# A saturating add in place of add and row ReLU in the inner feed-forward product, with every engine's queue put in a new order

## The chip, the cores and the metric

The kernel runs on one core of one Trainium2 chip. The metric is the device time of one execution in microseconds (us), the median of several runs. A core has TensorE (PE, matrix products into the PSUM banks; its weight loads are shown as PEld), VectorE (DVE), ScalarE (ACT), GpSimd (POOL) and SyncE (SP, which here only issues transfers).

## The reference

Two linear-attention blocks and two feed-forward blocks follow one another on x of 2048 rows by 512 columns; all tensors are bf16.

```python
def _A_ref(x, wqkv, wo):                      # 32 heads of 16
    qkv = (x @ wqkv) ...
    phi = lambda t: jnp.where(t > 0, t + 1, jnp.exp(t)) + 1e-6
    pq, pk = phi(q), phi(k)
    kv = jnp.einsum("bhsd,bhse->bhde", pk, v)
    z = jnp.einsum("bhsd->bhd", pk)
    num = jnp.einsum("bhqd,bhde->bhqe", pq, kv)
    den = jnp.einsum("bhqd,bhd->bhq", pq, z)[..., None] + 1e-6
    return (num / den) ... @ wo
def _B_ref(x, w1, w2):                        # w1 512x1376, w2 1376x512
    h = jnp.maximum(jnp.einsum("bsd,df->bsf", x, w1), 0)
    return jnp.einsum("bsf,fd->bsd", h, w2)
x = x + _A_ref(_layernorm(x), A_wqkv, A_wo)
x = x + _B_ref(_layernorm(x), B_w1, B_w2)     # then both once more
```

## The kernel before

The rows are 16 tiles of 128, taken in four chunks `t` of four tiles. Layers 0 and 2 are attention, layers 1 and 3 feed-forward. Everything stays in SBUF between layers.

**The queues.** The kernel is a list of about 1,640 small steps (`_Graph.add`), each with a name such as `pqs3_0`, its layer in front (`2.pqs3_0`), an engine, and the keys it reads and writes. A planner (`_list_schedule`) gives each engine its list. With `WINDOW` 1 on every engine, and the engine of each movable step fixed by an entry of `HINTS` whose name ends in `!`, an engine's list is simply its steps sorted by the index at which they were made plus their entry in `HINTS`. A queue is worked strictly in that order: a step that waits holds all behind it. Waits are on semaphores: a step waits for the steps that wrote what it reads or that read what it overwrites.

**Attention.** LayerNorm (`ln_stats`, `ln_norm`) gives `xn`; `tr…` are transposing transfers issued by SP into `Tb`, and for the first six tiles `trp…`/`trev…` transpose on PE and copy out. `kproj`, `qproj`, `qh` and, for many chunks, the Strassen form `k7`/`q7` (seven products for eight) make k and q; `_lin`, `_exp`, `_em`, `_phi` make phi of them; `g…`, `kv…`, `kvmask`, `m…` make the per-head matrix `Mf`, copied out by `gev…` and `mev…`. `wvless0` to `wvless3` subtract from the value weights their last row, which the load `ld_wvl` broadcast to all partitions. The denominator of chunk t is `den t` on PE, then `lnd t` (logarithm, L1222) and `rdc t` (exponential, L1224) on ACT, then four SP transfers `spread t_0..3` (L1234) that copy the reciprocals over the partitions, then two DVE products `pqs t_0`, `pqs t_2` (L1242) that scale q. `fin` (output product, 512 columns wide) of the chunk's four tiles waits for both; `resid` on DVE adds x.

**Feed-forward.** `b_h7` makes h of a chunk by a Strassen-Winograd form: products `h1` to `h7` for 2 or 1 pairs of column blocks at once (three groups `cs` per chunk: two wide, 512 columns of a PSUM bank, and one narrow, 256), results saved by ACT (`hv…`) or seeded into a second bank (L702). Two quarters of h are a bank's content clipped (`hc11`, `hc21`, ACT L1431 or DVE L1432); the other two, `hc12` and `hc22`, are a bank plus a saved product. The function `add` puts these two into the left and right half of one row of `big` (L1443, DVE) and, behind the second, clips the whole row in place: `hc22r` (ACT L1452 or DVE L1453). The last 96 columns are `hr`, clipped by `hrrelu` into a buffer that `ms_hr` set to zero on POOL, and transposed by `trh`. `b_out_sums` and `b_out` form the second product the same way; `p…` are its products.

Of the kernel before, what the change touches and what calls it, by code (L numbers as in the profile page):

```python
# [6 lines left out]

# [55 lines left out]
HINTS = {"0.aqsum1": -44, "0.aqsum1!": 0, "0.aqsum2": -5, "0.aqsum2!": 0, "0.aqsum3": -114, "0.aqsum3!": 0, "0.aqsum4": 0,  # L63
         "0.aqsum4!": 0, "0.as1": -12, "0.as1_2": -16, "0.as1_2!": 0, "0.as1_3": -37, "0.as1_3!": 0, "0.as2_2": 4,
         "0.as2_2!": 0, "0.as2_3": -26, "0.as2_3!": 0, "0.as3": -8, "0.as3_2": 30, "0.as3_2!": 0, "0.as3_3": 3,
         "0.as3_3!": 0, "0.as4_2": 17, "0.as4_2!": 0, "0.as4_3": -22, "0.as4_3!": 0, "0.as_h1": -11, "0.as_h2": -8,
         "0.as_id": 2, "0.bnag0": -4, "0.bnag1": -8, "0.bnag10": 37, "0.bnag11": 34, "0.bnag12": 8, "0.bnag13": 8,
         "0.bnag14": 7, "0.bnag15": -18, "0.bnag2": 1, "0.bnag3": 1, "0.bnag4": 5, "0.bnag5": 25, "0.bnag6": 6,
         "0.bnag7": 3, "0.bnag8": 36, "0.bnag9": 27, "0.bnst0": -6, "0.bnst1": -10, "0.bnst10": 27, "0.bnst11": 29,
         "0.bnst12": 2, "0.bnst13": -2, "0.bnst14": 2, "0.bnst15": -26, "0.bnst2": -3, "0.bnst3": -3, "0.bnst4": -2,  # L70
         "0.bnst5": 16, "0.bnst6": 2, "0.bnst7": -4, "0.bnst8": 23, "0.bnst9": 16, "0.den0": 11, "0.den1": 26,
         "0.den2": 17, "0.den3": -32, "0.fill0": 3, "0.fin0_0": -3, "0.fin0_2": 10, "0.fin10_0": -88, "0.fin11_0":
         -97, "0.fin12_0": -138, "0.fin13_0": -147, "0.fin14_0": -170, "0.fin15_0": -166, "0.fin1_0": -8, "0.fin1_2":
         4, "0.fin2_0": 4, "0.fin2_2": 0, "0.fin3_0": 6, "0.fin3_2": -6, "0.fin4_0": -8, "0.fin5_0": -28, "0.fin6_0":
         -12, "0.fin7_0": -36, "0.fin8_0": -95, "0.fin9_0": -87, "0.fnorm0": 1, "0.fnorm0!": 0, "0.fnorm1": -3,
         "0.fnorm1!": 0, "0.fnorm10": 43, "0.fnorm10!": 0, "0.fnorm11": 39, "0.fnorm11!": 0, "0.fnorm12": 17,
         "0.fnorm12!": 0, "0.fnorm13": 20, "0.fnorm13!": 0, "0.fnorm14": 10, "0.fnorm14!": 0, "0.fnorm15": 11,
         "0.fnorm15!": 0, "0.fnorm2": 6, "0.fnorm2!": 0, "0.fnorm3": 7, "0.fnorm3!": 0, "0.fnorm4": 35, "0.fnorm4!":
         0, "0.fnorm5": 54, "0.fnorm5!": 0, "0.fnorm6": 10, "0.fnorm6!": 0, "0.fnorm7": 6, "0.fnorm7!": 0, "0.fnorm8":
         47, "0.fnorm8!": 0, "0.fnorm9": 49, "0.fnorm9!": 0, "0.g0_0_0": 40, "0.g0_0_1": 8, "0.g0_0_2": -3,  # L80
         "0.g0_0_3": -31, "0.g0_1_0": 43, "0.g0_1_1": 14, "0.g0_1_2": 6, "0.g0_1_3": -28, "0.g0_2_0": 101, "0.g0_2_1":
         64, "0.g0_2_2": 23, "0.g0_2_3": -24, "0.g0_3_0": 12, "0.g0_3_1": 4, "0.g0_3_2": -20, "0.g0_3_3": -20,
         "0.g1_0_0": -11, "0.g1_0_1": -9, "0.g1_0_2": -9, "0.g1_0_3": -7, "0.g1_1_0": -9, "0.g1_1_1": -4, "0.g1_1_2":
         -3, "0.g1_1_3": 0, "0.g1_2_0": -71, "0.g1_2_1": -3, "0.g1_2_2": -1, "0.g1_2_3": -1, "0.gev0_0": -26,
         "0.gev0_0!": 0, "0.gev0_2": -22, "0.gev0_2!": 0, "0.gev1_0": -2, "0.gev1_0!": 0, "0.gev1_2": 2, "0.gev1_2!":
         0, "0.gevz": -12, "0.gevz!": 0, "0.k0_exp": -53, "0.k0_lin": -44, "0.k10_exp": -12, "0.k10_lin": -15,
         "0.k11_em": 10, "0.k11_exp": -22, "0.k11_lin": -38, "0.k11_phi": 21, "0.k12_em": -31, "0.k12_exp": -37,
         "0.k12_lin": -21, "0.k12_phi": -11, "0.k13_em": -44, "0.k13_exp": -47, "0.k13_lin": -37, "0.k13_phi": -28,
         "0.k14_em": -45, "0.k14_exp": -50, "0.k14_lin": -55, "0.k14_phi": -16, "0.k15_em": -63, "0.k15_exp": -67,
         "0.k15_lin": -62, "0.k15_phi": -24, "0.k1_em": 53, "0.k1_exp": -39, "0.k1_lin": -32, "0.k1_phi": 78,  # L90
         "0.k2_exp": -34, "0.k2_lin": -36, "0.k3_em": 55, "0.k3_exp": -29, "0.k3_lin": 6, "0.k3_phi": 58, "0.k4_exp":
         -46, "0.k4_lin": -15, "0.k5_em": 20, "0.k5_exp": 9, "0.k5_lin": 7, "0.k5_phi": 36, "0.k6_exp": -43,
         "0.k6_lin": -35, "0.k7_em": 1, "0.k7_exp": -17, "0.k7_lin": -32, "0.k7_phi": 40, "0.k8_exp": 24, "0.k8_lin":
         32, "0.k9_em": 28, "0.k9_exp": -18, "0.k9_lin": -21, "0.k9_phi": 33, "0.kproj0_0": -58, "0.kproj0_1": -56,
         "0.kproj10": -51, "0.kproj11": -47, "0.kproj12": -42, "0.kproj13": -53, "0.kproj14": -63, "0.kproj15": -73,
         "0.kproj1_0": -56, "0.kproj1_1": -52, "0.kproj2": -48, "0.kproj3": -42, "0.kproj4": -51, "0.kproj5": -16,
         "0.kproj6": -54, "0.kproj7": -48, "0.kproj8": -22, "0.kproj9": -30, "0.kv0_0": -25, "0.kv0_1": -24,
         "0.kv0_2": -24, "0.kv0_3": -20, "0.kv1_0": 1, "0.kv1_1": 1, "0.kv1_2": 4, "0.kv1_3": 4, "0.kvmask0": -22,
# [24 lines left out]
         "0.qc7_2_12_add": 22, "0.qc7_2_12_em": 30, "0.qc7_2_12_exp": 26, "0.qc7_2_12_phi": 33, "0.qc7_2_21_em": 51,
# [1858 lines left out]
```

## Time and profile before

| | |
|---|---|
| time, median of 3 runs (range) | 261.85 us (261.5 to 262.0) |
| span of the profiled execution, first to last instruction | 260.5 us |
| what the median has beside that span | 1.3 us |
| DVE busy | 230.8 us, 89% of the span, 572 instructions |
| ACT busy | 206.3 us, 79%, 446 instructions |
| POOL busy | 60.0 us, 23%, 163 instructions |
| transfers | 22.46 MB, mean 86 GB/s |

The profile is one execution. Times in its views are us from the start of the span; "mean" is ns of one instruction. [...]

### The profile page before, as it was taken

The numbers are of one execution on the slowest core, as the hardware profiler recorded it, in microseconds if no ns is written. First come the engines' busy times: TensorE is split into PE (matmuls) and PEld (weight loads), VectorE is DVE, ScalarE is ACT, GpSimd is POOL, SyncE is SP. The second block draws the span as 40 slices with busy tenths as digits, with TensorE's granted clock in tenths as the row PEclk, the third lists the DMA queues.
The fourth block names the chain that finished last, engine by engine and source line by source line (L and its number), as shares of the span: only waits on it lengthen the run. The fifth ranks groups of instructions, "written<-read, shape, count | busy, mean of one in ns | idle before, by whom it ended". The sixth has DMA issues, their size and how long they took to land.

```text
span 260.5 us, 5876 instructions
## 1 busy us (share of the span) xinstructions
PE 255.2 (98%) x2165; PEld 198.3 (76%) x2176; DVE 230.8 (89%) x572; ACT 206.3 (79%) x446; POOL 60.0 (23%) x163
## 2 busy tenths in 40 slices
PE   7999999999999999999999999999999999999995
PEld 3554577744788988889888878674388989888884
DVE  5999997799999999999989999858999998876684
ACT  4999999689999969999998899766899928853100
POOL 4100000037844015341420430003777000000000
PEclk9999999999999999999999999999999999999999
DMA  6767950754343062222130040057251414300104
GB/s 195 288 161 140 324 183 18 178 122 94 65 89 64 17 86 44 40 42 43 31 72 0 4 81 1 3 136 174 59 102 38 83 23 126 58 20 3 81 3 161
DMA packets 46268, 22.46 MB, mean 86 GB/s; under 512 B 35904, under 2 KB 44704, under 8 KB 46240
## 3 DMA queue, kind: packets, MB, share of 16 engines
q1 hardware_dynamic: 45968, 21.83, 34.8%
q10 hardware_dynamic: 272, 0.26, 0.4%
q8 instruction: 17, 0.28, 0.4%
q14 instruction: 11, 0.09, 0.1%
HBM read 7.14 MB, written 2.10 MB: 35 GB/s over the span
## 4 chain that ended last, share of the span: by engine, by line
PE 82%; DVE 5%; DMA 4%; SPq 4%; ACT 3%; issue 1%; DVEq 0%
PE ps L960 81%; SPq L1234 4%; DMA big<-rdc 3%; DVE xres L967 3%; DVE big L1242 1%; ACT lnd L1222 1%; DMA xin<-in_A_x_dram 1%; PE ps L919 1%; ACT rdc L1224 1%; DVE bst L851 0%; ACT big L1073 0%; DVE xin L1391 0%; PE ps L846 0%; ACT escr L1090 0%; ACT GT L1144 0%
## 5 line engine op out<-in xcount | busy, mean ns | idle before, releaser
L975 ACT ACTIVATE sqscr<-xres 128x512 bf16<-128x512 f32 x48 | 29.7, 621 | 4.4 <-DVE xres L967 3.0
L960 PE MATMUL ps<-w,big 128*128 128x256 bf16 (+1 forms) x256 | 32.6, 272 | 0.0
L960 PE MATMUL ps<-big,xn 128*128 128x256 bf16 (+1 forms) x221 | 31.6, 287 | 0.3
L702 ACT ACTIVATE ps<-ps 128x512 f32<-128x512 f32 (+1 forms) x41 | 22.7, 563 | 11.1 <-PE ps L960 11.1
L960 PE MATMUL ps<-Mf,big 128*128 128x512 bf16 x125 | 28.8, 379 | 0.7 <-DVE big L1242 0.5
L960 PEld LDWEIGHTS ps<-w,big 128*128 128x128 bf16 (+1 forms) x256 | 24.9, 98 | 3.1
L960 PEld LDWEIGHTS ps<-big,xn 128*128 128x128 f16 x224 | 21.5, 98 | 6.1 <-issue 0.7
L1443 DVE TENSOR_TENSOR big<-ps,escr 128x512 bf16<-128x512 f32 (+1 forms) x38 | 22.7, 600 | 3.6 <-PE ps L960 2.3
L960 PEld LDWEIGHTS ps<-Mf,big 128*128 128x128 bf16 x128 | 12.0, 98 | 15.8 <-DVE big L1242 2.0
L960 PE MATMUL ps<-Tb,w 128*128 128x256 f16 x160 | 23.7, 273 | 0.0
L960 PE MATMUL ps<-xn,xin 128*128 128x256 f16 x160 | 23.2, 273 | 0.0
L960 PE MATMUL ps<-xn,w 128*128 128x256 f16 x160 | 22.4, 273 | 0.0
L873 POOL TENSOR_SCALAR mean<-s 128x2 f32<-128x2 f32 x24 | 8.4, 350 | 56.0 <-DVE xres L967 53.5
L899 ACT ACTIVATE xn<-xres,nbias,rstd 128x512 f16<-128x512 f32 x26 | 20.7, 816 | 0.7 <-POOL nbias L883 0.6
L1462 ACT ACTIVATE escr<-ps 128x512 f32<-128x512 f32 (+1 forms) x38 | 19.2, 536 | 2.4 <-PE ps L960 2.3
L1431 ACT ACTIVATE big<-ps 128x512 bf16<-128x512 f32 (+1 forms) x38 | 19.0, 533 | 1.9 <-PE ps L960 1.8
L960 PE MATMUL ps<-wqkv,Tb 128*128 128x512 bf16 (+1 forms) x93 | 19.7, 342 | 0.1
L881 POOL TENSOR_TENSOR rstd<-veps,nhalf 128x2 f32<-128x2 f32 x24 | 18.4, 768 | 5.1 <-DVE veps L879 4.5
L960 PEld LDWEIGHTS ps<-Tb,w 128*128 128x128 bf16 x160 | 15.5, 98 | 2.5 <-DVE w L1391 0.4
L960 PE MATMUL ps<-w,Tb 128*128 128x96 bf16 (+2 forms) x176 | 17.3, 224 | 0.0
L960 PEld LDWEIGHTS ps<-xn,w 128*128 128x128 bf16 x160 | 15.4, 98 | 2.0
L960 PEld LDWEIGHTS ps<-xn,xin 128*128 128x128 bf16 x160 | 15.2, 98 | 2.0 <-DVE xres L967 0.2
(146 smaller groups left out, 626.1 us busy)
## 6 DMA issues: line engine op xcount, KB each, us to landing
big<-rdc SPq DMA_DIRECT2D x32, 128.0 KB, 2.7
w<-in_B_w_dram SPq DMA_DIRECT2D x1, 1376.0 KB, 7.2
w<-in_B_w_dram SPq DMA_DIRECT2D x1, 1280.0 KB, 10.4
xin<-in_A_x_dram SPq DMA_DIRECT2D x2, 512.0 KB, 6.5
wqkv<-in_A_wqkv_dram SPq DMA_DIRECT2D x3, 256.0 KB, 4.9
xin<-in_A_x_dram SPq DMA_DIRECT2D x4, 128.0 KB, 3.1
xin<-in_A_x_dram SPq DMA_DIRECT2D x2, 256.0 KB, 4.9
wqkv<-in_A_wqkv_dram SPq DMA_DIRECT2D x1, 512.0 KB, 4.1
```

Source lines behind the costliest of these rows:

```text
L702: g.add(ACT, lambda e: e.activation(psv[:, b, 0:w], psv[:, src, 0:w], ACTF.Identity), [("ps", src)], [("ps", b)], C_ACT_PSUM if w == 512 e ...
L873: g.add(POOL, lambda e: e.tensor_scalar(mean[:, sl], s1[:, sl], -INV_D, None, ALU.mult), [("s1", i) for i in tl], [("mean", i) for i in tl ...
L881: g.add(POOL, lambda e: e.tensor_tensor(rstd[:, sl], veps[:, sl], nhalf[:, 0:n], ALU.pow), [("veps", lo), ("nhalf",)], [("rstd", i) for i ...
L899: (ACT, lambda e: e.activation(xn[:, i, :], src, ACTF.Identity, scale=rstd[:, i:i + 1], bias=nbias[:, i:i + 1]), C_ACT_SB_AP)],
L919: last = e.transpose(psb()[:, 128 * q:128 * q + 128], xn[:, i, 128 * c:128 * c + 128], ident[:])
L960: last = e.matmul(o, l, r, start=st, stop=sp, skip_group_check=skip)
L967: g.add(DVE, lambda e: e.scalar_tensor_tensor(xres[:, i, :], psv[:, b, :], 0.0, src, ALU.add, ALU.add, accum_out=s1[:, i:i + 1]), [("ps", ...
L975: g.add(ACT, lambda e: e.activation(sqscr[:, q, :], xres[:, i, :], ACTF.Square, scale=math.sqrt(INV_D), accum_out=s2[:, i:i + 1]), xr(i), ...
L1234: dma(lambda e, j=j, u=u: e.dma_start(unit_ap(u), rdc[32 * j:32 * j + 32, t, :].unsqueeze(1).broadcast_to([32, 4, 512])), [("rdc", t)], [( ...
L1431: g.add_flex([(ACT, lambda e: e.activation(ap, src(), ACTF.Relu), C_ACT_PSUM if w == 512 else 270.0), (DVE, lambda e: e.tensor_scalar(ap, ...
L1443: g.add(DVE, lambda e: e.tensor_tensor(ap, sh(psv[:, bank, 0:w]), sh(other()), ALU.add), [("ps", bank)] + okeys + ([] if first else bk), q ...
L1462: g.add(ACT, lambda e, w=w: e.activation(q[:, 0:w], psv[:, bank, 0:w], ACTF.Identity), [("ps", bank)], key, C_ACT_PSUM if len(cs) == 2 els ...
```

## The change

In `add`, the DVE addition becomes one instruction `TENSOR_ADD_SAT`, which gives max(min(a + b, s0), s1); with s0 the largest f32 and s1 zero it is the sum, clipped. There is then no `hc22r`.

```diff
+from concourse import dve_ops
...
+        SPREADS = ((0,), (1,), (2,))
+        H_SAT = True
+        FMAX = 3.4028234663852886e38
...
-        FIRST_ACT_TILES = 4
+        RSTD_ACT = (0, 1, 2, 3, 6, 8, 12)
+        PE_TILES = 6
...
-                g.add_flex([(DVE, f, C_DVE_NORM_BF)],
+                g.add_flex([(DVE, f, C_DVE_NORM_BF)] + ([(POOL, f, C_POOL_NORM)] if i >= PE_TILES else []),
...
+                if H_SAT:
+                    g.add(DVE, lambda e: e._custom_dve(dve_ops.TENSOR_ADD_SAT, out=ap, in0=sh(psv[:, bank, 0:w]), in1=sh(other()), s0=FMAX, s1=0.0),
+                          [("ps", bank)] + okeys + ([] if first else bk), qk + (bk if first else []),
+                          C_DVE_PSUM if len(cs) == 2 else 335.0, name="%s_%d_%d" % (name, t, cs[0]))
+                    return
                 g.add(DVE, lambda e: e.tensor_tensor(ap, sh(psv[:, bank, 0:w]), sh(other()), ALU.add),
```

`RSTD_ACT`, `PE_TILES` and `SPREADS` have values that give the same steps as before; the merged form of the spreads that `a_spread` now allows is not used. `fnorm` of a later tile may go to POOL, and `fnorm9` does. `wvless` may go to POOL, but all four stay on DVE.

The rest of the diff replaces the whole table `HINTS` (1,907 entries become 1,796), and with it all five queues. 66 movable steps change engine. Among them, in layer 0: `trev2` and `gev0_0` from ACT to DVE, `mev0` from ACT to DVE and `mev1` back, `fnorm9` from DVE to POOL; in layer 2 `var4` and `veps4` from DVE to POOL; of the clips `hc11` and `hc21`, twelve wide and one narrow go from ACT to DVE and six wide and one narrow the other way. Stretches of the queues that differ (index plus hint, sorted):

| queue | before | after |
|---|---|---|
| PE, layer 0 | den0, g0_0_3, g0_1_3, g0_2_2, g0_2_3, q7_3_4, kv0_0, kv0_1, kv0_2, den2, den1 | den0, g0_0_3, g1_2_0, g0_2_3, g0_1_3, q7_3_4, den2, den1, g1_2_1, kv0_0, kv0_1, kv0_2 |
| ACT, layer 0 | lnd0, rdc0, gev0_0, gev0_2, qc7_3_22_exp, lnd2, rdc2, qc7_3_21_lin, lnd1, qc7_3_21_exp, rdc1 | lnd0, rdc0, gev0_2, lnd2, rdc2, qc7_3_22_exp, lnd1, rdc1 |
| DVE, layer 0 | pqs0_0, mev1, pqs2_2, aksum1, kvmask1, aksum2, aksum3, pqs2_0, pqs1_0, pqs1_2, resid1 | mev0, qc7_3_21_em, pqs2_2, qc7_3_21_phi, aksum1, kvmask1, aksum2, pqs2_0, aksum3, pqs1_0, pqs1_2, resid1 |
| DVE, layer 2 | pqs2_0, resid4, resid5, nbias0, resid7, resid6, var4, pqs3_0, veps4, nbias2, pqs3_2 | pqs2_0, resid4, resid5, nbias0, resid6, resid7, pqs3_0, pqs3_2, nbias2 |
| ACT, layer 2 | gevz, …, lnd0, rdc0, lnd1, rdc1, lnd2, rdc2 | the same |
| SP, layer 0 | ld_wv0, ld_wvl, tr2_1, tr2_0, tr3_1, tr3_0, ld_wo | ld_wv0, tr2_1, tr2_0, tr3_1, tr3_0, ld_wvl, ld_wo |
| DVE, layer 0 | the first step that reads ld_wvl is at place 51 (wvless3) | at place 73 (wvless2) |
| POOL, layer 0 | ms_hr among the first nine steps | ms_hr between nbias2 and norm3 |

Up to `wvless2` the DVE's new list holds, against the old list up to `as1_2`: in addition trev2, aqsum2, four sums (as1_2, as2_2, as1_3, as4_2), four wide `_em` (k5, k11, q1_1, q0_3), one single `_em` (k14) and four wide `_phi` (k5, k7, q0_1, k11); and not any more fnorm9, aqsum3 and wvless3.

More of the change, by code (lines that the diff above doesn't have):

```diff
@@ L60 @@
 WINDOW = {PE: 1, ACT: 1, DVE: 1, POOL: 1, SP: 1}
-HINTS = {"0.aqsum1": -44, "0.aqsum1!": 0, "0.aqsum2": -5, "0.aqsum2!": 0, "0.aqsum3": -114, "0.aqsum3!": 0, "0.aqsum4": 0,
[302 rows of a table removed]
+HINTS = {"0.aqsum1": -54, "0.aqsum2": -52, "0.aqsum3": 52, "0.aqsum4": 70, "0.as1": 46, "0.as1_2": -23, "0.as1_3": -51, "0.as2_2": -17, "0.as2_3": -7,
[219 rows of a table added]
 class _Op:
@@ L1116, in wv_less_last @@
             for m in range(4):
-                g.add(DVE, lambda e, m=m: e.tensor_tensor(wqkv[:, m, 2 * D:3 * D], wqkv[:, m, 2 * D:3 * D], wvl[:], ALU.subtract),
-                      [("wv0",), ("wvl",)], [("wv", m)], 335.0, name="wvless%d" % m)
+                f = (lambda e, m=m: e.tensor_tensor(wqkv[:, m, 2 * D:3 * D], wqkv[:, m, 2 * D:3 * D], wvl[:], ALU.subtract))
+                g.add_flex([(DVE, f, 335.0), (POOL, f, C_POOL_ADD)], [("wv0",), ("wvl",)], [("wv", m)], name="wvless%d" % m)
         def ones_col(lo, n):
@@ L1228, in rb_unit, with a_spread @@
             return 32 + 4 * j + t
-        def a_spread(t, first_layer):
-            late = 500.0 if first_layer and t == 0 else 0.0
+        def a_spread(t, n=1):
             for j in range(4):
                 u = rb_unit(t, j)
-                dma(lambda e, j=j, u=u: e.dma_start(unit_ap(u), rdc[32 * j:32 * j + 32, t, :].unsqueeze(1).broadcast_to([32, 4, 512])),
-                    [("rdc", t)], [("big", u)], 650.0, "spread%d_%d" % (t, j), issue=620.0, late=late)
+                dma(lambda e, j=j, u=u: e.dma_start(big[:, u * 512:(u + n) * 512],
+                                                    rdc[32 * j:32 * j + 32, t:t + n, :].rearrange("p n k -> p (n k)").unsqueeze(1)
+                                                    .broadcast_to([32, 4, 512 * n])),
+                    [("rdc", t + k) for k in range(n)], [("big", u + k) for k in range(n)], 650.0 * n, "spread%d_%d" % (t, j), issue=620.0)
         def a_pqs(t):
@@ L1676, in ln_first @@
             for i in range(4 * t, 4 * t + 4):
-                if t < FIRST_PE_CHUNKS and i < 6:
+                if i < PE_TILES:
                     ln_stats_first(i, [("xn", i - 2)] if 2 <= i < 4 else [])
@@ L1684, in ln_first @@
             if t == 1:
-                ln_part_first(6, 8)
-                ln_norm(6, True)
-                ln_norm(7, True)
-                tr_dma(1, 1)
+                for i in range(PE_TILES, 8, 2):
+                    ln_part_first(i, i + 2)
+                    ln_norm(i, True)
+                    ln_norm(i + 1, True)
+                    tr_dma(1, i // 2 - 2)
             if t >= FIRST_PE_CHUNKS:
@@ L1762, in pq @@
                         a_zc()
-                        for u in range(NCH - 1):
-                            a_den(u)
-                            a_spread(u, first_layer)
+                        for grp in SPREADS:
+                            for u in grp:
+                                a_den(u)
+                            a_spread(grp[0], len(grp))
                         if ("q", t) in A7[layer]:
@@ L1815, in p2 @@
                         a_den(NCH - 1)
-                        a_spread(NCH - 1, first_layer)
+                        a_spread(NCH - 1)
                         a_pqs(2)
```

2 lines of the change are left out of this document (1 added, 1 removed), and 521 rows, old and new, of the table HINTS.

## The prediction

> **What bounds the kernel now.** I read the page's busy lines and chain first, then the stages table over the two long feed-forward stretches, then PE's timeline.
>
> ```profile
> PE 255.2 (98%) x2165; PEld 198.3 (76%) x2176; DVE 230.8 (89%) x572; ACT 206.3 (79%) x446; POOL 60.0 (23%) x163
> ...
> PE 82%; DVE 5%; DMA 4%; SPq 4%; ACT 3%; issue 1%; DVEq 0%
> ```
>
> ```profile
> 70.00:150.00 80.00, 80.00 (x762) 71.14 (x760) 76.89 (x210) 72.79 (x155) 25.00 (x66) 1.00 0.24 45
> 190.00:250.00 60.00, 60.00 (x588) 53.62 (x587) 51.32 (x109) 38.37 (x82) 8.50 (x21) 1.00 0.24 54
> ```
>
> ```profile
> 19.89 1.03 PE L960 MATMUL ps<-wqkv,Tb 128*128 128x512 bf16 x4
> 167.28 1.03 PE L960 MATMUL ps<-big,xn 128*128 128x256 bf16 x8
> 61.70 2.15 PE L960 MATMUL ps<-Mf,big 128*128 128x512 bf16 x8
> 182.83 3.63 PE L960 MATMUL ps<-Mf,big 128*128 128x512 bf16 x16 [0.18 <-DVE big L1242]
> 186.76 3.41 PE L960 MATMUL ps<-Mf,big 128*128 128x512 bf16 x15 [0.30 <-DVE big L1242]
> ```
>
> ```profile
> L960 PE MATMUL ps<-Mf,big 128*128 128x512 bf16 x125 | 28.8, 379 | 0.7 <-DVE big L1242 0.5
> ```
>
> PE busy is the first column pair, the granted clock stands third from the end (1.00). In both stretches, where all the saturating adds lie, PE is busy throughout: 140 of 140 us. To see whether "busy" is real work I take start-to-start distances. Four 512-column products last 1.03 us and one is counted 0.379, so the distance is (1.03 - 0.379)/3 = 0.217 us; eight 256-column products give, with 0.27 for one, (1.03 - 0.27)/7 = 0.109. 588 products in 60 us are 0.102 on average, with the narrow ones among them. So PE streams there, and nothing is waited for.
>
> Where does PE wait? At 182.83 it is idle 0.18 us, at 186.76 0.30. As a product is counted 0.379 - 0.216 = 0.16 beyond its pace, PE really loses 0.34 and 0.46. At 61.70 eight products should last 7 x 0.217 + 0.379 = 1.90; they last 2.15, so 0.25 is lost too. These three, 1.05 us in all, are what a new order can win here. All three are behind `pqs`, DVE L1242.
>
> **The adds and the clips.**
>
> ```profile
> L1443 DVE TENSOR_TENSOR big<-ps,escr 128x512 bf16<-128x512 f32 x26 | 17.7, 684 | 1.9 <-PE ps L960 1.6
> L967 DVE SCALAR_TENSOR_TENSOR xres<-ps,xres 128x512 f32<-128x512 f32 x16 | 10.3, 686 | 0.1
> L1452 ACT ACTIVATE big<-big 128x1024 bf16<-128x1024 bf16 x7 | 7.4, 1059 | 0.9 <-DVE big L1443 0.9
> L1453 DVE TENSOR_SCALAR big<-big 128x1024 bf16<-128x1024 bf16 x9 | 3.8, 417 | 0.0
> L1452 ACT ACTIVATE big<-big 128x512 bf16<-128x512 bf16 x3 | 1.9, 640 | 2.3 <-DVE big L1443 2.3
> L1453 DVE TENSOR_SCALAR big<-big 128x512 bf16<-128x512 bf16 x5 | 1.4, 285 | 0.0
> L1432 DVE TENSOR_SCALAR big<-ps 128x512 bf16<-128x512 f32 x7 | 4.8, 682 | 0.0
> ```
>
> Removed are 24 row clips: ACT 7.4 + 1.9 = 9.3 us, DVE 3.8 + 1.4 = 5.2 us. The queues give part of it back: a net six wide bank clips go to DVE, 6 x 0.68 = 4.1 us by the L1432 row, and leave ACT. So ACT loses its 9.3 us and six clips more, and DVE about 1 us. On the time this is worth nothing by itself: PE, 140 of 140 us busy, does as many products as before. What the clips cost was hidden behind PE, and so is what replaces them. The sums `ssum` of `b_out_sums`, which read the finished rows, can start a clip earlier; they feed `p…` products, for which PE did not wait in either stretch, so that too is worth nothing there.
>
> The saturating add has no row. From below: an add that costs less than the plain one is excluded as far as rows go, since plain and two-operation instructions of this shape from PSUM have one price, 684 and 686 ns. From above: add and clip one behind the other, 684 + 682 = 1.37 us, 0.68 more. I take 0.68 us, no extra, because the nearest row is that of two operations in one pass. The point from which it decides: in 70 to 150 DVE has 80 - 76.9 = 3.1 us free; of the 5.2 us freed some 2.2 lie there (of layer 1's clips four wide and two narrow were DVE's), and of the bank clips that change engine a net two wide come and one narrow goes, some 1.0 more to do. That leaves 4.3 us for 16 wide and 8 narrow adds, about 20 wide ones: 0.2 us each. Above 0.9 us per wide add DVE becomes the bound.
>
> **The new order in layer 0.** The chain in order of time (start, us, what):
>
> ```profile
> 45.18 0.61 ACT lnd L1222
> ...
> 51.53 2.60 DMA big<-rdc
> ...
> 54.15 0.69 DVE big L1242
> ...
> 61.11 1.66 DVE big L1242 x2
> ...
> 62.81 2.76 PE ps L960 x12
> ```
>
> ```profile
> 44.30 0.50 PE L960 MATMUL ps<-GT,wqkv 128*128 128x128 bf16 x6
> 44.73 0.61 PE L960 MATMUL ps<-big,Zc 128*32 128x512 bf16 x8
> 43.39 1.05 ACT L1154 ACTIVATE GT<-ps 128x512 bf16<-128x512 f32 x2
> 44.34 0.71 ACT L1090 ACTIVATE escr<-big,nbexp 128x512 bf16<-128x512 bf16 x1
> 52.72 2.12 DVE L1242 TENSOR_TENSOR big<-big 128x1024 bf16<-128x1024 bf16 x3
> ```
>
> `den2` moves ahead of `kv0_0` to `kv0_2`, six products, so it starts at 44.30, not 44.73. `lnd2` moves ahead of `gev0_0` (now on DVE) and of `qc7_3_22_exp`, the steps at 43.39 and 44.34, so ACT is free for it. `rdc2` and the eight SP issues behind it come 0.43 earlier, and so do the last landing (54.13) and `pqs1_2`. But DVE, in order, gains only what it waits: three `pqs` at a pace of 0.61 would end after 2 x 0.61 + 0.69 = 1.91 and take 2.12, so 0.21. From there `resid` and `pqs3` run without a hole to 62.77, and PE's 0.25 falls to 0.04. Gain 0.21, bounds 0 (another step is late) and 0.25. What DVE takes on there, `gev0_0`, costs up to 0.68 (as the L1432 row, a read of a full bank); it lies in the time before `kvmask0`, the next DVE step that needs PE, and if that cover is gone it costs its own length. The four spreads of a chunk go out in another order, which changes the last landing by nothing: there are four either way.
>
> **The new order in layer 2.**
>
> ```profile
> 182.08 0.69 DVE L1242 TENSOR_TENSOR big<-big 128x1024 bf16<-128x1024 bf16 x1 [1.01 <-DMA big<-rdc]
> ...
> 185.20 0.16 DVE L877 TENSOR_TENSOR var<-s,nm 128x2 f32<-128x2 f32 x1
> 185.28 0.69 DVE L1242 TENSOR_TENSOR big<-big 128x1024 bf16<-128x1024 bf16 x1
> 185.88 0.16 DVE L879 TENSOR_SCALAR veps<-var 128x2 f32<-128x2 f32 x1
> 185.95 0.15 DVE L883 TENSOR_TENSOR nbias<-mean,rstd 128x2 f32<-128x2 f32 x1
> 186.02 0.68 DVE L1242 TENSOR_TENSOR big<-big 128x1024 bf16<-128x1024 bf16 x1
> ```
>
> `var4`, `veps4` and `nbias2` no longer stand in front of `pqs3_2`: 0.08 + 0.07 + 0.07, so 0.22 us of PE's 0.46. The first wait, 0.34 at 182.83, stays: it is set by the landing of chunk 2's spreads at 182.06, whose ACT and SP order is unchanged. The statistics that are put off wait on POOL, which nothing near needs.
>
> **Other moves.**
>
> ```profile
> 14.10 0.53 SPq L799 DMA_DIRECT2D wvl<-in_A_wqkv_dram  x1
> 17.80 7.22 SPq L904 DMA_TRANSPOSE Tb<-xn  x4
> ...
> 24.82 0.42 DVE L1029 TENSOR_TENSOR big<-Tb 128x512 f16<-128x512 f16 x1
> ```
>
> ```profile
> w<-in_B_w_dram SPq DMA_DIRECT2D x1, 1376.0 KB, 7.2
> ...
> wvl<-in_A_wqkv_dram SPq DMA_DIRECT2D x1, 128.0 KB, 3.8
> ```
>
> `ld_wvl` goes behind four transposes, to 25.0, and lands at 25.0 + 3.8 = 28.8. DVE reaches its first reader `wvless2` at: 24.82 (`as1_2` now) plus the steps added, 15 of them. A DVE step of 0.69 us is followed after 0.60 (185.28 above), so one of 0.42 after 0.34: ten of those are 3.4, four `_phi` of 0.61 are 2.4, the single `_em` 0.2; 6.0, less the three that go, 1.0, so 29.8. Cover 1.0 us; cost 0. Behind it on DVE stand `q0_3_phi`, `as3_2` and the k9 pair, whose results PE reads.
>
> ```profile
> L926 DVE COPY Tb<-ps 128x512 f16<-128x512 f16 x1 | 0.4, 424 | 0.2 <-PE ps L919 0.2
> L827 POOL MEMSET hr<- 128x1024 bf16 x1 | 1.0, 951 | 0.0
> ```
>
> `trev2` on DVE holds the norms behind it for 0.34 to 0.42, and `kproj2` reads it; ACT's copy at the same place was not free either, so I take 0, with -0.1 to 0.42 as bounds. `ms_hr` in front of `norm3` holds that norm, then its transpose on SP, then `hr0` and `hs1` of chunk 0, for up to 0.95. PE has the rest of `fin` and `h1` to do before it reads them, so 0, bounds 0 and 0.95. `fnorm9` on POOL gives DVE 0.3 back; the chain it is in ends in a transpose with the same cover as the load above.
>
> **The sum.** 0.21 + 0.22 = 0.43 us of 260.5, so a span of 260.1; with the 1.3 that the median has beside the span, 261.4.
>
> **The rivals.** *More waits go* (chance 0.23): chunk 2's spreads in layer 2 land earlier, and all three waits, 1.05 us, vanish: 260.8; with waits of the first microseconds down to 260.2. For it: ACT is over 9 us lighter; against it: that chain runs behind PE, not behind ACT's clips. *PE has room* (0.02): if 512-column products could follow closer than the 0.217 us of the row, 70 to 150 would be DVE's, 76.9 of 80 us and about 1 less after the change, so some 4 us less, and 190 to 250 shorter by as much at the least: about 254. [...] *The waits stay* (0.08): another step is late in the same place, 261.85. *The load of the last value row comes late* (0.12), slower: if it takes the 7.2 us of the w row, as w1 and w2 are issued just behind, it lands at 32.2, 2.4 after DVE gets there; all of DVE's queue, the `_phi` and `as` steps that PE's next products read, is held. From 1.0 us of delay it decides; at 7.2 it costs 2.4 - 0.4 = 2.0 net, 263.9. *The add is dear* (0.14), slower: at the upper bound 20 x 0.68 = 13.6 us in layer 1 against 4.3 free, so 9 us there, up to about 271 if layer 3 hides its own; at 1.0 us per add some 2 us, 263.5.
>
> **How the numbers follow.** The forecast has 0.41 and its own range is 261.1 to 261.6. About 0.2% (0.5 us) can be told from no change here, so the line lies at 261.3, inside that range: 0.20 of it counts as faster, 0.21 as the same. Faster: 0.20 + 0.23 + 0.02 = 0.45. Same: 0.21 + 0.08 = 0.29. Slower: 0.12 + 0.14 = 0.26. The range runs from 260.4, all three waits and some early ones, to 262.8, into the late load and a slightly dear add, and leaves out the rest of those two.
>
> **What would show it.** Right: the saturating add's row at 0.68 us; PE's row at 61.7 without the lost 0.25; `pqs3_0` and `pqs3_2` back to back and an idle under 0.15 before the last `fin`; 70 to 150 still full. Wrong: DVE idle before `wvless2` with the load as releaser; adds of 0.9 us or more; a PE wait behind a bank that DVE clips late.

## The result: slower by 0.5%, mostly through one wait

After: 263.35 us (median of 9 runs, 262.87 to 263.67); before: 261.85 in the same session (9 runs). The ratio is 1.005, 95% interval 1.0036 to 1.0065. Forecast was 261.4, with 262.8 as the upper end of the range, so the sign and the range were both missed. One kernel of this study, that of experiment 4, had four of its twelve executions at 267.7 to 270.3 us and a granted clock of 0.987 to 0.994; its ratio to before counts the other eight alone (median 261.5), and as none of the four was profiled, what made them long is open.

From the page of after: the busy line, then the chain that ended last, by engine and by line.

```profile
PE 255.0 (98%) x2166; PEld 199.2 (76%) x2176; DVE 231.7 (89%) x572; ACT 194.9 (75%) x426; POOL 68.9 (26%) x159
...
PE 87%; DVE 4%; issue 3%; ACT 3%; DMA 2%; POOL 1%
PE ps L882 86%; DVE bst L773 2%; DMA Tb<-xn 1%; DVE xn L811 1%; DMA xin<-in_A_x_dram 1%; POOL hm L757 1%; ACT escr L864 1%; ACT xres L864 1%; ACT big L862 1%; ACT Tb L847 0%; PE ps L841 0%; PE ps L768 0%; DVE mv L774 0%; ACT rstd L781 0%; DVE KVT L1088 0%
```

What the change meant to do has happened: ACT is 11.4 us lighter (206.3 to 194.9). DVE is not (230.8 to 231.7), as other steps moved to it. PE still sets the end. New on the chain is POOL with one line, L757. That is `as_h1`, which builds a constant mask and which the prediction does not name. (Lines of after are about 78 lower: PE's products are L882, `pqs` is L1165, the saturating add L1367.) The stages table over the two feed-forward stretches, then the groups that answer to those of before:

```profile
70.00:150.00 80.00, 80.00 (x763) 71.38 (x761) 76.42 (x208) 67.55 (x149) 24.26 (x65) 1.00 0.29 48
190.00:250.00 60.00, 60.00 (x584) 53.25 (x583) 51.83 (x109) 33.22 (x75) 10.10 (x22) 1.00 0.27 57
```

```profile
L1367 DVE CUSTOM_DVE_ANT_0 big<-ps,escr 128x512 bf16<-128x512 f32 x26 | 17.7, 687 | 2.0 <-PE ps L882 1.5 <-ACT escr L1390 0.3
L882 PE MATMUL ps<-Mf,big 128*128 128x512 bf16 x126 | 28.5, 379 | 0.1
L882 PE MATMUL ps<-big,xn 128*128 128x512 bf16 x28 | 7.5, 379 | 1.9 <-POOL xn L1043 1.7
```

The saturating add costs 687 ns, the plain one 684. Both stretches are full, 140 of 140 us. The idle time in front of the `fin` products fell from 0.7 to 0.1 us. The loss is in the last row: 1.7 us of idle time in one place, behind POOL. PE's timeline, then POOL's, then DVE's around it:

```profile
29.81 0.60 PE L882 MATMUL ps<-big,xn 128*128 128x256 bf16 x4
32.11 1.47 PE L882 MATMUL ps<-big,xn 128*128 128x512 bf16 x8 [1.71 <-POOL xn L1043]
```

```profile
23.25 0.23 POOL L1043 MEMSET xn<- 128x4 f16 x1 [4.03 <-DMA Tb<-xn]
23.30 8.69 POOL L757 TENSOR_SCALAR_AFFINE_SELECT hm<-onesf 128x32 f32<-128x32 f32 x1
31.94 0.11 POOL L1043 MEMSET xn<- 128x4 f16 x1
31.99 0.81 POOL L753 TENSOR_SCALAR_AFFINE_SELECT bmask<-m1f 128x128 bf16<-128x128 f32 x1
```

```profile
23.00 0.42 DVE L870 TENSOR_SCALAR escr<-escr 128x1024 bf16<-128x1024 bf16 x1
23.34 0.69 DVE L872 TENSOR_TENSOR big<-big,escr 128x1024 bf16<-128x1024 bf16 x1
...
31.10 0.43 DVE L951 TENSOR_TENSOR big<-Tb 128x512 f16<-128x512 f16 x1
31.44 0.43 DVE L870 TENSOR_SCALAR escr<-escr 128x1024 bf16<-128x1024 bf16 x1
31.90 0.69 DVE L872 TENSOR_TENSOR big<-big,escr 128x1024 bf16<-128x1024 bf16 x1
```

In the new POOL list `as_h1` stands in front of `onec4`, the MEMSET (L1043) of the column of ones beside v of tiles 4 to 7, which PE's `g0_3_1` reads. The four products at 29.81 should have been followed after 4 x 0.109 = 0.43 us, at 30.24; the next one starts at 32.11, so PE loses 1.87 us. The same `as_h1` took 0.26 us in before, at the start of the program (POOL's timeline of before):

```profile
1.66 0.26 POOL L835 TENSOR_SCALAR_AFFINE_SELECT hm<-onesf 128x32 f32<-128x32 f32 x1
```

What did it wait for during 8.69 us? Look at the ends of DVE's rows. From 23.34 on, 20 instructions in a row each start 84 to 95 ns before the one in front has ended (23.34 against 23.00 + 0.42). The first that starts later than that is at 31.90, 35 ns behind the end of its forerunner (31.44 + 0.43 = 31.87): it is `k9_phi`, which reads what `k9_em` directly in front of it wrote. POOL's instruction ends 0.1 us later. The theory for the experiments (A) is therefore: a POOL instruction that reads SBUF is held while DVE's SBUF instructions follow each other without a hole, and all of POOL's list behind it is held too.

### The profile page after: what moved, and what is told of

Same layout as the page of the kernel before. It is cut to its first block, busy times and chain, and to the rows that moved or that the text cites. A ratio compares the mean times of both kernels' runs of the same rounds, so it can differ in the third digit from the quotient of the medians.

```text
span 261.5 us, 5847 instructions
## 1 busy us (share of the span) xinstructions
PE 255.0 (98%) x2166; PEld 199.2 (76%) x2176; DVE 231.7 (89%) x572; ACT 194.9 (75%) x426; POOL 68.9 (26%) x159
## 4 chain that ended last, share of the span: by engine, by line
PE 87%; DVE 4%; issue 3%; ACT 3%; DMA 2%; POOL 1%
PE ps L882 86%; DVE bst L773 2%; DMA Tb<-xn 1%; DVE xn L811 1%; DMA xin<-in_A_x_dram 1%; POOL hm L757 1%; ACT escr L864 1%; ACT xres L864 1%; ACT big L862 1%; ACT Tb L847 0%; PE ps L841 0%; PE ps L768 0%; DVE mv L774 0%; ACT rstd L781 0%; DVE KVT L1088 0%
## 5 line engine op out<-in xcount | busy, mean ns | idle before, releaser
L882 PE MATMUL ps<-big,xn 128*128 128x256 bf16 (+1 forms) x220 | 31.8, 286 | 1.9 <-POOL xn L1043 1.7
L624 ACT ACTIVATE ps<-ps 128x512 f32<-128x512 f32 (+1 forms) x41 | 22.1, 547 | 15.3 <-PE ps L882 14.3
L882 PE MATMUL ps<-w,big 128*128 128x256 bf16 (+1 forms) x256 | 32.5, 272 | 0.0
L882 PE MATMUL ps<-Mf,big 128*128 128x512 bf16 x126 | 28.5, 379 | 0.1
L882 PEld LDWEIGHTS ps<-big,xn 128*128 128x128 f16 x224 | 21.2, 98 | 8.5 <-POOL xn L1043 2.0
L882 PEld LDWEIGHTS ps<-w,big 128*128 128x128 bf16 (+1 forms) x256 | 25.0, 98 | 3.0
L1354 ACT ACTIVATE big<-ps 128x512 bf16<-128x512 f32 (+1 forms) x32 | 16.1, 514 | 12.1 <-PE ps L882 11.9
L1367 DVE CUSTOM_DVE_ANT_0 big<-ps,escr 128x512 bf16<-128x512 f32 (+1 forms) x38 | 22.7, 602 | 2.4 <-PE ps L882 1.9
L882 PE MATMUL ps<-Tb,w 128*128 128x256 f16 x160 | 24.0, 273 | 0.0
L882 PE MATMUL ps<-xn,w 128*128 128x256 f16 x160 | 23.7, 272 | 0.0
L882 PEld LDWEIGHTS ps<-Mf,big 128*128 128x128 bf16 x128 | 12.2, 98 | 14.5 <-ACT Mf L1095 0.5
L882 PE MATMUL ps<-xn,xin 128*128 128x256 f16 x160 | 23.0, 272 | 0.0
L882 PE MATMUL ps<-wqkv,Tb 128*128 128x512 bf16 (+1 forms) x94 | 19.7, 343 | 0.1
L821 ACT ACTIVATE xn<-xres,nbias,rstd 128x512 f16<-128x512 f32 x24 | 18.8, 807 | 0.5 <-DVE nbias L805 0.3
L882 PE MATMUL ps<-w,Tb 128*128 128x96 bf16 (+2 forms) x176 | 17.3, 224 | 0.0
L882 PEld LDWEIGHTS ps<-Tb,w 128*128 128x128 bf16 x160 | 15.5, 98 | 2.2 <-DVE w L1314 0.2
L882 PEld LDWEIGHTS ps<-xn,xin 128*128 128x128 bf16 x160 | 15.6, 98 | 1.9
L882 PEld LDWEIGHTS ps<-xn,w 128*128 128x128 bf16 x160 | 15.4, 98 | 1.9
```

What stands on the lines that cost most here:

```text
L624: g.add(ACT, lambda e: e.activation(psv[:, b, 0:w], psv[:, src, 0:w], ACTF.Identity), [("ps", src)], [("ps", b)], C_ACT_PSUM if w == 512 e ...
L821: (ACT, lambda e: e.activation(xn[:, i, :], src, ACTF.Identity, scale=rstd[:, i:i + 1], bias=nbias[:, i:i + 1]), C_ACT_SB_AP)],
L882: last = e.matmul(o, l, r, start=st, stop=sp, skip_group_check=skip)
L1354: g.add_flex([(ACT, lambda e: e.activation(ap, src(), ACTF.Relu), C_ACT_PSUM if w == 512 else 270.0), (DVE, lambda e: e.tensor_scalar(ap, ...
L1367: g.add(DVE, lambda e: e._custom_dve(dve_ops.TENSOR_ADD_SAT, out=ap, in0=sh(psv[:, bank, 0:w]), in1=sh(other()), s0=FMAX, s1=0.0), [("ps", ...
```

## The experiments

The kernel before ran beside each of them on the same chip; its median was 261.76 (first four), 262.04 (next four), 261.99 (9 and 10) and 262.02 (11 and 12). The four groups ran on different chips, so versions of different groups are compared by their ratios to before. All moves are entries of `HINTS`.

### 1. All constants back at POOL's front

```diff
-"0.as1": 46, "0.as_h1": 149, "0.as3": 155, "0.ms_nbexp": 162, "0.as_h2": 176, "0.ms_hr": 413
+"0.as1": -12, "0.as_h1": -11, "0.as3": -8, "0.ms_nbexp": -10, "0.as_h2": -8, "0.ms_hr": -1
```

> After, with the six constant steps of POOL (as1, as_h1, as3, as_h2, ms_nbexp, ms_hr) back at the front of its queue, where before has them; nothing else moved. Theory A (the loss inside the span is as_h1 standing in front of onec4 on POOL): the AFFINE_SELECT takes 0.26 us again, PE's wait of 1.7 us at 30.3 is gone and the span falls by 1.87 us, from 261.5 to 259.6 or 259.7; with the 1.75 us that after has beside its span, 261.4 us. Rival B (something else would have held PE there a little later, the wait only hid it): span above 260.5, time above 262.2. Rival C (the place of the constants does not matter): 263.35.

Measured: 261.93 us, ratio to before 1.0 (0.9987 to 1.0013), span 260.1, no wait at 30 us. The loss is gone, so rivals B and C fall. The 261.4 was not reached: PE's wait of 0.24 us at about 63 us is back, which after does not have. Experiment 11 comes to that.

### 2. Only `as_h1` moved, behind `onec12`

```diff
-"0.as_h1": 149
+"0.as_h1": 177
```

> After, with as_h1 alone moved, behind onec12; as3, which also reads SBUF on POOL, then stands behind onec4 as in after. Theory A (a POOL instruction that reads SBUF is held as long as DVE's SBUF instructions follow each other without a hole, and what stands behind it is held too): onec4 is done at 23.4, PE's wait at 30.3 is gone, as3 is held in as_h1's place from 23.4 to the first hole of DVE at about 31.9, so it takes about 8.5 us, and onec12 comes at about 32; 261.4 us as in the run with the constants in front, up to 261.9 if onec12 is then late for its reader. Rival (as_h1 itself is slow at that place, whatever runs on DVE): as3 takes 0.35 to 0.8 us, the long AFFINE_SELECT is as_h1 again, behind onec12; the time is 261.4 too.

POOL's timeline of this run, then PE's:

```profile
23.60 8.73 POOL L753 TENSOR_SCALAR_AFFINE_SELECT bmask<-m1f 128x128 bf16<-128x128 f32 x1
32.28 0.10 POOL L748 MEMSET nbexp<- 128x2 f32 x1
32.31 0.11 POOL L1043 MEMSET xn<- 128x4 f16 x1
32.36 0.62 POOL L757 TENSOR_SCALAR_AFFINE_SELECT hm<-onesf 128x32 f32<-128x32 f32 x1
```

```profile
30.08 1.90 PE L882 MATMUL ps<-big,xn 128*128 128x256 bf16 x12
```

Measured: 261.54 us, ratio 0.9993 (0.9973 to 1.0013). `as3`, another instruction, is held in the same place for 8.73 us, and `as_h1` is cheap elsewhere: it is the place, not the instruction. PE no longer waits, as `onec4` is in front of the held one. One step moved behind four others (`onec4`, `as3`, `ms_nbexp`, `onec12`) takes the ratio to before from 1.005 to 0.9993, about 1.5 us.

### 3. The saturating add alone, in the old order

```diff
-g.add(DVE, lambda e: e.tensor_tensor(ap, sh(psv[:, bank, 0:w]), sh(other()), ALU.add),
+g.add(DVE, lambda e: e._custom_dve(dve_ops.TENSOR_ADD_SAT, out=ap, in0=sh(psv[:, bank, 0:w]), in1=sh(other()), s0=3.4028234663852886e38, s1=0.0),
...
-qk = qk + first_half[0]
+g.gone += 1; return
```

(`gone` is added to the index of all later steps, so that the old entries of the table give the old order without the `hc22r`.)

> Before with the saturating add and without the row clips, every queue otherwise in the old order. Price of the add by its row: 0.687 us as in after. The span should stay at 260.5 (PE sets the end and waits at the same three places). Theory D (the 0.43 us that after has more beside its span, 1.75 against 1.3, comes with the saturating add): 262.2 to 262.3 us. Rival (it comes with something else in the new kernel): 261.85 us.

```profile
L1443 DVE CUSTOM_DVE_ANT_0 big<-ps,escr 128x512 bf16<-128x512 f32 x26 | 17.7, 685 | 2.9 <-PE ps L960 2.2 <-ACT escr L1462 0.3
```

Measured: 262.07 us, ratio 1.0008 (0.9994 to 1.0021): no difference. The half of the change that the title speaks of is worth nothing either way. Theory D falls as well: this run's profiled execution took 262.32 with a span of 260.6, 1.72 beside it, and the runs of before on this chip have as much (261.97 with a span of 260.2). In all executions on record the distance lies between 1.69 and 1.82. So the 1.3 us that the prediction took was a median of some executions less the span of another, longer one.

### 4. Before, with `as_h1` between `onec8` and `onec4`

```diff
-"0.as_h1": -11, "0.onec4": 52, "0.as_h2": -8
+"0.as_h1": 152, "0.onec4": 96, "0.as_h2": 184
```

> Before with three POOL steps in the order of after: onec8, as_h1, onec4, onec12, as_h2; nothing else moved. In before DVE's starts follow each other without a hole from 20.1 to 35.4 us, all of them reading SBUF. Theory A (held until DVE's first hole): as_h1 starts at about 22.6 and is held beyond 31; PE waits from 30.7 (g0_3_1, the first product that reads onec4's column) until the want of products makes a hole in DVE's stream, 1.2 to 4.7 us; time 263.0 to 266.5. Rival E (a fixed cost of this instruction late in the program, 8.7 us, say code that has to be fetched): it ends at 31.3, PE waits 0.6 us, 262.4. Rival F (it costs 0.3 us here and only in after's surroundings more): 261.85.

POOL's rows, then DVE's:

```profile
22.58 0.37 POOL L835 TENSOR_SCALAR_AFFINE_SELECT hm<-onesf 128x32 f32<-128x32 f32 x1
22.91 0.96 POOL L1121 MEMSET xn<- 128x4 f16 x1
27.10 0.12 POOL L1121 MEMSET xn<- 128x4 f16 x1 [3.22 <-DMA Tb<-xn]
27.14 8.60 POOL L838 TENSOR_SCALAR_AFFINE_SELECT hm<-hm 128x32 bf16<-128x32 f32 x1
```

```profile
21.78 1.37 DVE L889 TENSOR_SCALAR xn<-xin,mv,rstd 128x512 f16<-128x512 bf16 x4
23.07 0.75 DVE L948 TENSOR_SCALAR escr<-escr 128x1024 bf16<-128x1024 bf16 x2
...
35.54 0.68 DVE L1075 TENSOR_TENSOR big<-ps,lnd 128x512 bf16<-128x512 f32 x1
```

Measured: 261.67 us (all twelve executions, see the result), ratio 0.9993 (0.9978 to 1.0007). The time that was expected is missed: by the time and by `as_h1`'s 0.37 us it is rival F that came true. The rows then sharpen the theory. `as_h1` slipped through in 0.37 us, although DVE had no hole: DVE was at its norms, one SBUF tensor each at 512 elements per (1.37 - 0.41)/3 = 0.32 us. The MEMSET behind it met the `_em` steps, 1,024 elements per 0.33 us, and took 0.96 instead of 0.11. And `as_h2`, at 27.14, was held for 8.60 us by `_em`s, `_phi`s and sums, until DVE came at 35.54 to an instruction whose first operand is in PSUM; it ended 0.2 us into that one. So the 0.37 us stands beside norms, and the 8.60 beside `_em`s (one SBUF tensor, 1,024 elements in 0.33 us), `_phi`s (two, 1,024 in 0.60) and sums (two, 512 in 0.33), none of which was tried alone; and the end fits a hole (in after, 35 ns at 31.90) or an instruction of another kind (here at 35.54). It is not peculiar to after, as rival F would have it: `as_h2` is held in before's own stretch. Rival E, a fixed 8.7 us, falls with the 0.37.

### 5. A hole in DVE's stream, POOL untouched

```diff
-"0.k7_phi": 11
+"0.k7_phi": 0
```

> After with one DVE step moved: k7_phi directly behind k7_em, whose result it reads, three places earlier. POOL's queue is untouched: as_h1 still stands in front of onec4. A DVE step that reads the result of the one directly in front of it starts about 35 ns behind that one's end instead of 80 ns before it (20.70 and 31.90 in after), so this makes a hole in DVE's stream at about 24.7 us. Theory A (POOL's reading instruction is held until such a hole): the AFFINE_SELECT ends at about 24.8 instead of 31.99 and takes 1.5 us instead of 8.69; onec4 follows, PE's wait of 1.87 us at 30.3 is gone, 261.4 to 261.8 us, although DVE itself loses 0.12 us. Rivals (a fixed cost of the instruction, or a port that is shared evenly in time): 8.7 us or nearly, 263.3 us.

POOL's rows, DVE's, and PE's:

```profile
23.48 1.51 POOL L757 TENSOR_SCALAR_AFFINE_SELECT hm<-onesf 128x32 f32<-128x32 f32 x1
24.95 0.11 POOL L1043 MEMSET xn<- 128x4 f16 x1
25.00 0.81 POOL L753 TENSOR_SCALAR_AFFINE_SELECT bmask<-m1f 128x128 bf16<-128x128 f32 x1
...
26.88 0.83 POOL L760 TENSOR_SCALAR_AFFINE_SELECT hm<-hm 128x32 bf16<-128x32 f32 x1
```

```profile
24.45 0.42 DVE L870 TENSOR_SCALAR escr<-escr 128x1024 bf16<-128x1024 bf16 x1
24.91 0.69 DVE L872 TENSOR_TENSOR big<-big,escr 128x1024 bf16<-128x1024 bf16 x1
...
26.57 0.41 DVE L951 TENSOR_TENSOR big<-big,Tb 128x512 f16<-128x512 f16 x1
26.91 0.68 DVE L872 TENSOR_TENSOR big<-big,escr 128x1024 bf16<-128x1024 bf16 x1
27.51 0.49 DVE L870 TENSOR_SCALAR escr<-escr 128x1024 bf16<-128x1024 bf16 x1
```

```profile
30.09 1.90 PE L882 MATMUL ps<-big,xn 128*128 128x256 bf16 x12
```

Measured: 261.65 us, ratio 0.9991 (0.9965 to 1.0017). DVE's start at 24.91 comes 34 ns behind the end of `k7_em`, and POOL's instruction is through: 1.51 us, as expected, for 8.69. Making DVE's own list worse, by two dependent steps one behind the other, takes the ratio from 1.005 to 0.9991 and makes the kernel about 1.5 us faster. A fixed cost, or a sharing that is even in time, would have left it at 8.7 or nearly. But a hole is not the only way out: `as3` at 25.00 and `as_h2` at 26.88, which both read, are through in 0.81 and 0.83 us although DVE's starts overlap there as before (26.91 against 26.57 + 0.41), and the DVE instruction at 27.51 takes 0.49 for 0.42. Why POOL got in between two DVE instructions here, and not in 20 tries in after, no run shows.

### 6. A write-only instruction in the same place

```diff
-"0.as_h1": 149
+"0.as_h1": -11, "0.probe": 147
...
+g.add(POOL, lambda e: e.memset(prb[:], 0.0), [], [("prb",)], 100, name="probe"); g.gone -= 1
```

> After with as_h1 at the front of POOL's queue and, in the place that it left in front of onec4, a MEMSET of an unused tile of the same shape (128x32 f32), which writes SBUF and reads nothing. [...] Rival (anything on POOL is held there): the MEMSET takes 8.5 us, PE waits 1.8 us, 263.3.

```profile
22.67 0.22 POOL L762 MEMSET prb<- 128x32 f32 x1
22.73 0.19 POOL L1043 MEMSET xn<- 128x4 f16 x1
22.78 8.67 POOL L753 TENSOR_SCALAR_AFFINE_SELECT bmask<-m1f 128x128 bf16<-128x128 f32 x1
```

Measured: 261.49 us, ratio 0.9973 (0.9952 to 0.9994); the forecast against the rival's 263.3 was 261.4 to 261.8. The MEMSET is done in 0.22 us, the next instruction that reads is held for 8.67. In this place it is the reading one that is held; the MEMSET of 0.96 us beside two `_em` steps in experiment 4 shows that a write is not free beside every DVE instruction.

### 7, 9, 10 and 12. Looking for a version that beats both

After has two small PE waits that before lacks, 0.2 us each: at 14.0 `kproj4` waits for ACT's copy of tile 4, at 25.1 `kproj14` is early for chunk 3. The entries moved:

```diff
 # 7
-"0.as_h1": 149, "0.kproj4": -63, "0.k3_em": 30
+"0.as_h1": 177, "0.kproj4": -58, "0.k3_em": 36
 # 9 (10: this, with the constants of experiment 1)
-"0.as_h1": 149, "0.kproj4": -63, "0.k5_em": -9
+"0.as_h1": -11, "0.kproj4": -58, "0.k5_em": -6
 # 12: as 9, and
-"0.q7_2_1": -3
+"0.q7_2_1": -45
```

> After with as_h1 behind onec12 and two steps moved for the two new PE waits of about 0.2 us that after has and before has not: kproj4 behind qh0_1_1_0 (it waited for ACT's copy of tile 4 at 14.0), and k3_em behind fnorm14 on DVE, so that the transposes of the last four tiles can start up to 0.3 us earlier (kproj14 waited for their landing at 25.1). Theory (these two waits are what the new order lost in the first 30 us besides POOL's): the run with as_h1 behind onec12 was 261.54; 0.2 to 0.4 us less, 261.15 to 261.35. Rival (the places are made up elsewhere, PE meets the next late input): 261.5.

> After with three steps moved: as_h1 to the front of POOL's queue, kproj4 behind qh0_1_1_0, and k5_em on DVE from in front of fnorm12 to directly behind it (fnorm12 is the last norm that the transposes of chunk 3 wait for; the earlier try with k3_em made DVE wait for ACT's rstd instead and PE's wait at 25.3 grew to 0.50 us). Theory: fnorm12 ends 0.33 us earlier, both PE waits of 0.2 us (14.0, 25.1) are gone; against the kernel before, PE has the wait at 62.3 (0.25) less and no new one: 261.1 to 261.3 us, a ratio of 0.997 to 0.998. Rival (waits of the first 12 us and of landings, which differ from run to run, are all that is left): 261.5, no difference from the run in which only as_h1 was moved.

> The same with all six constant steps of POOL at the front, as in before. Theory (the front costs nothing, POOL is idle there; the 0.4 us between the run with all constants in front, 261.93, and the one with as_h1 behind onec12, 261.54, was landings): the same time as the run with three moves, within 0.2 us. Rival (the constants in the first three microseconds, or hr cleared there, cost something): 0.3 to 0.4 us more.

> The run with three moves (as_h1 to the front, kproj4 behind qh0_1_1_0, k5_em behind fnorm12) and a fourth: q7_2_1, four products of 0.109 us, in front of kproj14, as before had it in front of its chunk-3 products. In the run with three moves PE waited 0.35 us there, because the last transposes go out only when rstd12 of ACT is there. Theory: 0.43 us of work covers it, the wait is gone; 261.1 to 261.3 us, 0.3% under before. Rival (the step is late for the products behind it): 261.5.

PE's rows in 7, in 9, and in 12:

```profile
25.99 2.75 PE L882 MATMUL ps<-wqkv,Tb 128*128 128x512 bf16 x12 [0.33 <-ACT escr L864]
```

```profile
24.98 2.76 PE L882 MATMUL ps<-wqkv,Tb 128*128 128x512 bf16 x12 [0.19 <-DMA Tb<-xn]
```

```profile
25.61 2.76 PE L882 MATMUL ps<-wqkv,Tb 128*128 128x512 bf16 x12 [0.37 <-ACT big L862]
...
30.64 1.91 PE L882 MATMUL ps<-big,xn 128*128 128x256 bf16 x12 [0.55 <-ACT big L862]
```

Measured: 261.67 (0.9962 to 1.0001), 261.57 (0.9976 to 1.0018), 261.69 (0.9978 to 1.0019) and 262.59 us (1.0 to 1.0037). The wait at 14.0 is gone in all of them and turns up again, longer, at 25: behind ACT's reading of a bank, behind the last transposes, and with the fourth move behind ACT in two places. By these rows ACT and the transposes limit that stretch together, and a PE that arrives earlier only waits longer. The rivals of 7 and 9 (261.5) were right; 12 came out 1.1 us above its rival's 261.5, and whether its two waits behind ACT are all of that is not shown. Of all versions tried, only that of experiment 6 lies below before with its whole interval, and 2 and 9, which have the same cure, do not; so no version is shown to beat before. That 10 is within 0.2 us of 9, as it was expected, says that constants at the front cost no more than that there.

### 8. Before once more

> The kernel before, unchanged, profiled once more. If PE's waits behind the products that scale q (0.25 us at 62.3, 0.34 and 0.46 at 182 to 187 in the profile that the prediction was made from) belong to the kernel, they stand there again with the same lengths. If they belong to single executions, whose transfers of the reciprocals land up to half a microsecond apart, the two in layer 2 are shorter or gone (no other profile of this study shows them), and the one at 62.3 has another length.

PE's waits in this execution, then its timeline in layer 2:

```profile
PE ps L960 <- DVE KVT L1166: 0.9, 1, 0.9
PE ps L960 <- DMA wqkv<-in_A_wqkv_dram: 0.7, 1, 0.7
```

```profile
179.70 10.52 PE L960 MATMUL ps<-Mf,big 128*128 128x512 bf16 x48
```

One time, 263.42 us with a span of 261.7. In layer 2, 48 products take 47 x 0.216 + 0.379 = 10.53 us: no wait at all. The 0.34 and 0.46 us at 182 to 187, of which the prediction meant to win 0.22, belonged to the one execution that it was made from; none of the other profiles of this study has them, four with this order of layer 2 among them (3, 4, 8, 11). In their stead this execution waited 0.7 us for a load and 0.9 for the masked product `KVT`. The wait at 62 us did come again, with the same length: 0.245.

### 11. `ms_hr` alone, in the kernel before

```diff
-"0.ms_hr": -1
+"0.ms_hr": 414
```

> Before with one POOL step moved: ms_hr, a MEMSET of 0.95 us, from the front of POOL's queue to directly in front of norm3, where after has it. In every profile with ms_hr at the front POOL's norm3 (1.27 us) starts at the same time as DVE's pqs3_0 and pqs3_2, the second of which then takes 1.09 us instead of 0.69, and PE waits 0.24 us or more at about 62; in every profile with ms_hr in front of norm3 the pair takes 1.29 and PE does not wait there. Theory G (POOL's reading norm holds DVE's product of two SBUF inputs; it was ms_hr, and not the earlier den2 and lnd2, that took the wait away): the pair takes 1.29 us, the wait at 62.3 is gone, 0.25 us less in the span; time 261.5 to 261.7 against 261.85. Rival H (the wait went with den2 and lnd2, as the prediction had it): the second product takes 1.09 us still, or the wait stays.

POOL's and DVE's rows of before, then of this run:

```profile
60.95 1.27 POOL L894 TENSOR_SCALAR xn<-xres,mean,rstd 128x512 f16<-128x512 f32 x1
61.02 1.73 DVE L1242 TENSOR_TENSOR big<-big 128x1024 bf16<-128x1024 bf16 x2
```

```profile
61.43 0.94 POOL L827 MEMSET hr<- 128x1024 bf16 x1
62.37 1.11 POOL L894 TENSOR_SCALAR xn<-xres,mean,rstd 128x512 f16<-128x512 f32 x1
...
61.55 1.29 DVE L1242 TENSOR_TENSOR big<-big 128x1024 bf16<-128x1024 bf16 x2
```

Here POOL is the one that holds. In before `norm3`, which reads, collides with `pqs3_0` and `pqs3_2`; the pair takes 1.73 us, 0.44 more than 1.29, and PE waits 0.25. With the write-only `ms_hr` in between, `norm3` comes when the pair is under way, the pair takes 1.29 and PE's wait is gone. `den2` and `lnd2` stand as in before, so rival H falls. Through the whole study the split is clean: with `ms_hr` at the front (before, twice, and 1, 3, 4, 10) the pair takes 1.72 to 1.78, with `ms_hr` in front of `norm3` (after, 2, 5, 6, 7, 9, 11, 12) 1.29. In the time it does not show: 262.07 us, ratio 0.9997 (0.9976 to 1.0019), where theory G gave 261.5 to 261.7. A quarter of a microsecond is far less than single executions differ by (261.0 to 263.3 in this run).

## Why the prediction was wrong, point by point

**The bound.** Right: PE sets the end, the feed-forward stretches are full, and only waits count.

**The add and the clips.** Right: 687 ns against 684, and worth nothing (experiment 3). The dear add and PE having room are refuted (four 512-column products last 1.03 us in after too, at 28.94). That DVE would be about 1 us lighter was wrong, it is 0.9 heavier: the sum took the clips and not the other steps that changed engine. No wait hangs on it.

**Layer 0, 0.21.** The size was right by luck, the mechanism wrong. The wait at 62 us did go (0.25), but not because `den2` and `lnd2` came earlier; experiments 1 and 10 have these moves and keep the wait. It went with `ms_hr`, which the prediction had listed as a possible cost of up to 0.95 ("holds that norm"). The row that would have shown it stood in the prediction's chain: `61.11 1.66 DVE big L1242 x2`, where two products at their pace take 1.29.

**Layer 2, 0.22.** The waits were real in the profiled execution and in no other profile. The sum subtracted them from a time, 261.85, that did not hold them: that execution's own time was not 260.5 + 1.3 but, by the distance between time and span in the other runs (1.69 to 1.82), about 260.5 + 1.75 = 262.25. With the right distance the same sum gives 261.8, no difference.

**Other moves, 0.** This is the step that failed: it left a term out of the sum, without a reason. It names `ms_hr` as the POOL step that moves, and says nothing of `as_h1`, which the new table puts 160 places of the index later, in front of `onec4`. What a moved step holds up behind it was asked for SP's load and not for POOL's constants. Even listed, it would have been priced at 0.26 by the row at 1.66, and at POOL's 23.30 that is a cover of 6.7 us until `g0_3_1`; the price of a POOL step that reads depends on what DVE does at that moment (`as_h1` took 0.26, 0.37, 0.62, 1.51 and 8.69 us in before, 4, 2, 5 and after). Measured 8.69, so 1.87 on PE. Of the rest, `ld_wvl` was in time (`wvless2` at 30.17 waited for nothing), and `fnorm9` on POOL took 2.22 us without a wait behind it. The two PE waits of 0.2 at 14.0 and 25.1 were not foreseen; experiments 7 to 12 took the first away and only made the second longer.

**The account.** 1.87 - 0.25 + 0.2 + 0.2 gives 2.0 us more; measured are 1.5. With the hold out of the way of `onec4` the ratios to before lie between 0.9973 and 1.0 (experiment 12, with a wait of its own, aside), against 1.005; so the hold itself is worth 1.3 to 2.0 us, and the other terms can't be told from the differences between executions.

## What to carry to other kernels

Before a reading POOL step is moved, read DVE's rows at its new place: if each starts before the one in front has ended (by 84 to 95 ns in after), and they are like the `_em`s, `_phi`s and sums here (1,024 elements of one SBUF tensor in 0.33 us, or two SBUF tensors), the step can be held, for 8.60 to 8.89 us in five runs, and all behind it in POOL's list with it. It need not be: in experiment 5 two such steps were through in 0.81 and 0.83 us, and no run shows what decides. So put such steps where POOL and DVE are idle (0.26 us for `as_h1` at 1.66 in before, with DVE idle from 1.18 to 2.99), and steps that others need in front of them. And before a wait is booked as a gain, see it in a second profile of the same kernel.

## What the runs showed of the hardware

POOL instructions of 0.26 to 0.35 us (`as_h1`, `as_h2` and `as3` at the start of before) took 8.60 to 8.89 us next to a busy DVE in five runs (8.69 in after, 8.73, 8.60, 8.67 and 8.89 in experiments 2, 4, 6 and 7), and `as_h1` took 1.51 where a hole of 34 ns came early (experiment 5). In after the hold went on across 20 DVE instructions in a row and ended 0.1 us into `k9_phi`, which starts behind a hole of 35 ns; in experiment 5 `as_h2` (26.88) was through in 0.83 us, beside two DVE instructions. An instruction that only writes took 0.22 us in the place where a reading one took 8.67 (experiment 6), and 0.96 beside two `_em` steps (experiment 4). The hold goes both ways: beside POOL's norm in before a DVE product of 0.69 us lasted 1.09, the pair 1.73 for the 1.29 of experiment 11. What property of the two instructions makes a hold, and which of the two then waits, is not shown. The kernel's planner has no such hold for POOL steps whose names begin with `as`, and gives them fixed prices of 260 to 350 ns; that this is why the new order put them there is not shown either.
